# New places in PSUM for the values' sums, the gate's product and the transposes of an attention loop

## The chip, the cores and the metric

The kernel runs on 1 core of a Trainium2 chip. The metric is the device time of one execution in microseconds. Before the change it is 406.52 us, the median of 3 runs (405.61 to 407.78).

## The reference

Three layers follow each other: attention with a bias computed from positions, a mixture of experts with one expert per token, and a two-layer network with the gate h * cos(h). What matters here is the attention and the choice of the expert:

```python
scores = q @ k.T / sqrt(64) + bias                # 2 sequences, 8 heads, 576 x 576
attn = softmax(scores)                            # exp(scores - max) / (sum + 1e-9)
x = attn @ v                                      # rows of 512: 8 heads of 64
logits = x @ w_gate                               # 8 experts
gate_w = softmax(logits)[argmax]                  # one weight per row
out[i] = gate_w[i] * expert(x[i])
```

## The kernel before

**Tiling.** The attention is done in 36 steps. A step is one block of 128 query rows and one pair of heads; four steps make a block, and there are nine blocks (four of each sequence, and one in which each sequence has 64 rows). Steps are software-pipelined by hand: `step_of(n)` (line 804) issues, in this order on each engine, work of several steps. Per step n:

- `emit_exp(n, 1)` (L402, ScalarE): the exponential of the second head's scores;
- `emit_qk(n + 1, 0)` and `emit_qk(n + 1, 1)` (L385, TensorE): the next step's scores for the first and the second head, then `emit_sum` (L393, VectorE), which adds the bias and takes the minimum;
- `emit_tr(n, 0..2)` (L416, TensorE): nine 128x128 blocks of the exponentials are transposed in three groups of three, and `emit_tev(n, 0..2)` (L423, ScalarE) copies each group to SBUF; between the second and the third group stands `emit_nat(n - 2)` (L460), one more transpose, which `emit_nrm(n - 2)` (L467, VectorE) reads;
- `run_late`: pieces of the routing of a finished block (see below); `go_on` ends what they began;
- `bias_half(g, 0)` (L341 TensorE, L342 ScalarE): half of a group of rows of the bias for a later block, in steps 0 to 25; the passes L317 of VectorE (L315 of ScalarE in the first steps) prepare it;
- `emit_exp(n + 1, 0)` (L402), then in steps 27 to 31 a conversion of weights (L705, ScalarE);
- `emit_pv(n - 1)` (L434, TensorE): the values' sums, and `emit_xs(n - 1)` (L444, ScalarE), the copy of them to SBUF;
- `bias_half(g, 1)`.

**The eight PSUM banks** of the loop. Line 217 allocates `xb`, `bb`, `t0`, `t1`, one bank each, and line 220 the two score tiles `sa` and `sb`, two banks each (one for each half of 288 score columns; columns 288 to 511 of each bank are unused). `next_s` hands `sb` to the first head and `sa` to the second. `next_t` hands `t0` and `t1` in turn to the groups of transposes, so with three groups per step the third takes the bank of the first. The fourth quarter of such a bank takes the transpose of `emit_nat`, and the small products of the routing (`late_ps`). `xb` holds the values' sums, in two slots that alternate by step, and the gate's product of `f1` beside them (columns 256 to 383). `bb` holds the bias halves, and after the last of them, from step 25 on, the products of the routing (`own`).

**The routing of a block** (`finish_block`, line 494): `f1` multiplies by the gate's weights (L503 TensorE, L505 ScalarE), `f2` transposes the result and finds the best expert (L509, L512 to L522), `f3` takes the exponential (L536, ScalarE), and `f4` computes the gate's weight (L542, L543, VectorE) and multiplies the 512 columns of the rows with it (L549, VectorE). They wait in the list `late`; `run_late` (line 663) takes one piece a step before `emit_tev(n, 2)`, and `f3` and `f4` ahead of the next piece. For the first eight blocks this falls inside the loop (`f4` in steps 7, 11, 15, 20, 24, 27, 31 and 33), for the last one behind it, where `aux[0]` has become VectorE. Then `route` sends the rows to the experts' lists (L600, GpSimd).

At the end of step 34 `part_banks` gives the four score banks to the experts' sums; in step 35 `turned` transposes the first expert's rows into them.

Of the kernel before, what the change touches and what calls it, by code (L numbers as in the profile page):

```python
# [14 lines left out]
AF = mybir.ActivationFunctionType  # L15
ALU = mybir.AluOpType
# [7 lines left out]
DM = H * D  # L24
# [78 lines left out]
def attention_moe_kernel(  # L103
    ctx: ExitStack, tc: tile.TileContext,
    qd, kd, vp, small, ttab, wg, mw1, mw2, win, wout, out, dbg=None,
):
    nc = tc.nc
    V, A, P, T, Y = nc.vector, nc.scalar, nc.gpsimd, nc.tensor, nc.sync
# [85 lines left out]
    HS = S // 2  # L194
# [22 lines left out]
    xb, bb, t0, t1 = (banks.tile([128, 512], F32, name=n) for n in ("xb", "bb", "t0", "t1"))  # L217
    sst = ExitStack()
    scores = sst.enter_context(tc.tile_pool(name="scores", bufs=1, space=PSUM))
    s_bank = [scores.tile([128, 2, 512], F32, name=n) for n in ("sa", "sb")]  # L220
    t_bank = [t.rearrange("p (a c) -> p a c", a=4) for t in (t0, t1)]
    hp_w, acc_w, hp, acc = [], [t0, t1, bb], [], []

    def part_banks():
# [4 lines left out]
        hp.extend(t[:, 0:CAP] for t in hp_w)  # L229
        acc.extend(t[:, 0:CAP] for t in acc_w)  # L230

    turn_ = {"s": 0, "t": 0}

    def next_s():
        turn_["s"] += 1
        return s_bank[turn_["s"] % 2]

    def next_t():
        turn_["t"] += 1
        return t_bank[turn_["t"] % 2]  # L240

    def consts():
        of = cut(0, 128)
# [34 lines left out]
    def v_of(b, p, a, n):  # L278
        for lo, hi, t in v_parts[b, p]:
            if lo <= a and a + n <= hi:  # L280
                return t[:, a - lo:a - lo + n]
# [83 lines left out]
    e_t, et_t, z_t, xs_t, xn_t, rz_t = {}, {}, {}, {}, {}, {}  # L365
    qk_t, mn_t, tp_t, spare = {}, {}, {}, {}
# [6 lines left out]
    def emit_qk(n, u, with_sum=True):  # L373
        b, ib, p = steps[n]
        h = 2 * p + u
        if u == 0:
            if p == 0:
                z_t[b, ib] = sm_p.tile([128, H], F32, tag="z", name="z")
            e_t[n] = e_p.tile([128, 2, S], F32, tag="e", name="e")
            mn_t[n] = sm_p.tile([128, 2], F32, tag="mn", name="mn")  # L380
        ps = next_s()
        for c, a, e in [(c, 64 * c, 64 * c + 64) for c in range(B)] if b == BOTH else [(b, 0, 128)]:
            for half in range(2):
                rows_ = slice(64 * half, 64 * half + 64)
                T.matmul(out=ps[a:e, half, 0:HS], lhsT=qt[b, ib][rows_, h, a:e], rhs=kt[c, p][rows_, u, :], start=True, stop=True)  # L385
        ps_of[n, u] = ps
        if with_sum:
            emit_sum(n, u)
# [18 lines left out]
    def emit_tr(n, g):  # L407
        b, ib, p = steps[n]
        if g == 0:
            et_t[n] = et_p.tile([128, 9, 128], F32, tag="et", name="et")  # L410
        src = e_t[n].rearrange("p u s -> p (u s)")
        spare[g] = next_t()
        ps = spare[g]
        for j in range(3):
            blk = 3 * g + j
            T.transpose(ps[:, j, :], src[:, 128 * blk:128 * blk + 128], ident[:, :])  # L416
        tp_t[n, g] = ps
        if g == 2:
            e_t.pop(n)

    def emit_tev(n, g):
        dst, ps = et_t[n][:, 3 * g:3 * g + 3, :], tp_t.pop((n, g))
        A.activation(out=dst, in_=ps[:, 0:3, :], func=AF.Copy)  # L423

    def emit_pv(n):
        b, ib, p = steps[n]
        et = et_t[n]
        et_t.pop(n)
        for c, a, e in [(c, 64 * c, 64 * c + 64) for c in range(B)] if b == BOTH else [(b, 0, 128)]:
            xo = xb[:, 128 * (n % 2) + a:128 * (n % 2) + e]  # L430
            for j in (4, 0, 1, 2, 3):
                for i in range(4):
                    u, at_ = i // 2, 512 + 32 * i if j == 4 else 64 * (4 * (i // 2) + j) + 32 * (i % 2)
                    T.matmul(  # L434
                        out=xo[32 * i:32 * i + 32], lhsT=v_of(c, p, at_, 32),
                        rhs=et[:, 4 if j == 4 else 5 * u + j, a:e], start=(j == 4), stop=(j == 3),
                    )
        if p == 0:
            xs_t[b, ib] = xs_buf[n // NP % 2]
            xn_t[b, ib] = rows[tile_of(b, ib)]  # L440

    def emit_xs(n):
        b, ib, p = steps[n]
        A.activation(out=xs_t[b, ib][:, p, :], in_=xb[:, 128 * (n % 2):128 * (n % 2) + 128], func=AF.Copy)  # L444

    def emit_rz(n):
        b, ib, p = steps[n]
# [29 lines left out]

        return [(5 * c + t, 64 * c, 64 * c + 64) for c in range(B)] if b == BOTH else [(t, 0, 128)]

    aux = [P]  # L480
    own = []

    def late_f1():
        return own[0][:, 0:128] if own else xb[:, 256:384]

    def late_ps():
        return own[0][:, 128:256] if own else spare[0][:, 3]
# [6 lines left out]
    def finish_block(b, ib):  # L494
        t = tile_of(b, ib)
        loc = {}

        xs, row, rz = xs_t[b, ib], xn_t[b, ib], rz_t[b, ib]

        def f1():  # L500
            ps = late_f1()
            for p in range(NP):
                T.matmul(out=ps[32 * p:32 * p + 32, :], lhsT=wgs[:, p, :], rhs=xs[:, p, :], start=True, stop=True)  # L503
            yield
            A.activation(out=lt_buf[:, :], in_=ps[:, :], func=AF.Copy)  # L505

        def f2():
            ps = late_ps()
            T.transpose(ps, lt_buf[:, :], ident)  # L509
            yield  # L510
            lp = sm_p.tile([128, H, E], F32, tag="lp", bufs=1, name="lp")
            V.tensor_tensor(  # L512
                out=lp.rearrange("p (q u) e -> p q u e", u=2),
                in0=ps.rearrange("p (q z e) -> p q z e", q=NP, e=E)[:, :, 0:2],
                in1=rz.rearrange("p (q u) -> p q u", u=2)[:, :, :, None].to_broadcast([128, NP, 2, E]), op=ALU.mult,
            )
            lg = sm_p.tile([128, E], F32, tag="lg", name="lg")
            V.tensor_reduce(out=lg, in_=lp.rearrange("p h e -> p e h"), axis=AX.X, op=ALU.add)
            top = sm_p.tile([128, 8], F32, tag="top", bufs=2, name="top")
            V.max(out=top, in_=lg)  # L520
            ix = sm_p.tile([128, 8], U32, tag="ix", bufs=2, name="ix")
            V.max_index(out=ix, in_max=top, in_values=lg)  # L522
            nm = sm_p.tile([128, 1], F32, tag="nm", bufs=2, name="nm")
            aux[0].tensor_scalar(out=nm, in0=top[:, 0:1], scalar1=-1.0, scalar2=None, op0=ALU.mult)  # L524
            for t_, a, e in parts_of(b, t):
                aux[0].tensor_copy(idxf[a:e, t_:t_ + 1], ix[a:e, 0:1])
                aux[0].tensor_scalar(
                    out=oh[a:e, t_, :], in0=eio[a:e, 0:E], scalar1=idxf[a:e, t_:t_ + 1], scalar2=None, op0=ALU.is_equal,
                )
            loc.update(lg=lg, nm=nm)  # L530

        def f3():
            lg, nm = loc["lg"], loc["nm"]
            ex = sm_p.tile([128, E], F32, tag="ex", bufs=2, name="ex")
            es = sm_p.tile([128, 1], F32, tag="es", bufs=2, name="es")
            A.activation(out=ex, in_=lg, func=AF.Exp, bias=nm, scale=1.0, accum_out=es)  # L536
            loc["es"] = es

        def f4():
            es = loc["es"]  # L540
            gt = sm_p.tile([128, 1], F32, tag="gt", bufs=2, name="gt")
            V.tensor_scalar(out=gt, in0=es, scalar1=1e-9, scalar2=None, op0=ALU.add)  # L542
            V.reciprocal(out=gt, in_=gt)  # L543
            P.memset(row[:, DM:RW], 0.0)
            word = row[:, DM:DM + 1].bitcast(I32)
            P.iota(word, pattern=[[0, 1]], base=128 * ib if b == BOTH else b * S + 128 * ib, channel_multiplier=1)
            if b == BOTH:
                P.tensor_scalar(out=word[64:128], in0=word[64:128], scalar1=S - 64, scalar2=None, op0=ALU.add)
            V.tensor_scalar(out=row[:, 0:DM], in0=row[:, 0:DM], scalar1=gt[:, 0:1], scalar2=None, op0=ALU.mult)  # L549
            for t_, a, e in parts_of(b, t):  # L550
                row_t[t_] = row

        late.extend([(1, f1), (1, f2)] + [(0, f3)] + [(1, choose)] * ((b, ib) == CHOOSE) + [(0, f4)])
# [119 lines left out]
        return rest_  # L673

    def go_on(rest_):
        for g in rest_:
            next(g, None)

# [107 lines left out]
    ns = len(steps)  # L786
# [17 lines left out]
    def step_of(n):  # L804

        g, nxt = RUNS.get(n), RUNS.get(n + 1)
# [3 lines left out]
        if n > 1:  # L810
            b, ib, p = steps[n - 2]
# [8 lines left out]
        if n + 1 < ns:  # L820
            b, ib, p = steps[n + 1]
# [17 lines left out]
        emit_tr(n, 2)  # L839
        begun = run_late(LATE_B.get(n, n < LATE_FROM))  # L840
        emit_tev(n, 2)
        if nxt is not None:
            bias_h(nxt, on_act=ON_ACT if n < ACT_TO else (), quads=(0, 1))
        if n in EARLY:
# [20 lines left out]
        if n == SOONER:  # L865
            b, ib, p = steps[n - 1]
# [131 lines left out]

    for n in range(ns):
        step_of(n)  # L1000
    spare[1] = next_t()
    assert not late
    emit_nat(ns - 2)
    emit_rz(ns - 1)
# [5 lines left out]
        emit_nat(ns - 1)  # L1010
        emit_nrm(ns - 1)

    spare[1] = xb.rearrange("p (a c) -> p a c", a=4)
    b, ib, p = steps[ns - 1]
    finish_block(b, ib)
    tile_done(b, ib)
# [410 lines left out]
```

## Time and profile before

| | |
|---|---|
| median of 3 runs | 406.52 us (405.61 to 407.78) |
| profiled execution, its own time | 409.39 us |
| its span, first to last instruction | 407.3 us |
| mean granted TensorE clock | 0.985 |
| TensorE matmuls, weight loads | 375.4 us (92%), 288.3 us (71%) |
| VectorE, ScalarE, GpSimd | 293.9 us (72%), 282.3 us (69%), 48.0 us (12%) |
| attention loop, first scores of step 1 to those of step 34 | 28.04 to 198.15 us |

PE is TensorE's matmuls, PEld its weight loads, DVE VectorE, ACT ScalarE, POOL GpSimd. L416 is line 416 of the kernel before. In a timeline a row has the start and the duration in microseconds, the engine, line and operation, the tile written and those read, their shapes, the number of instructions merged, and in brackets the engine's idle time before it with what ended it. Matmuls are pipelined and their ends modelled.

### The profile page before, as it was taken

The page shows a single profiled execution, that of the slowest core. Times are in us where ns is not written, and L with a number is a line of the kernel's source. Part 1 is how long each engine was busy: PE and PEld are TensorE (multiplying, and loading weights), DVE is VectorE, ACT ScalarE, POOL GpSimd, SP SyncE. Part 2 cuts the span into 40 slices and gives each one's busy share as a digit, 9 for nine tenths or more (in the row PEclk, how much of TensorE's full clock was granted, in tenths as well). Part 3 has the DMA queues.
Part 4 walks back from the last instruction along what each step waited for, and adds up shares of the span by engine and source line. Part 5 has one row for each costly group of instructions (what it writes and reads, how often), then busy time and mean ns, then how long its engine had stood idle before and what let it go on. Part 6 is the DMA issues. An engine that isn't in the chain of part 4 may idle for free. (4 is left out here: it accounts for less than half of the span.)

```text
span 407.3 us, 10577 instructions
## 1 busy us (share of the span) xinstructions
PE 375.4 (92%) x4106; PEld 288.3 (71%) x4106; DVE 293.9 (72%) x759; ACT 282.3 (69%) x633; POOL 48.0 (12%) x122
## 2 busy tenths in 40 slices
PE   8888989999999999999978989998999999899992
PEld 5335656666666666767767879964998998789971
DVE  3856566868687967589766968974687788888670
ACT  3858978888888778899864448734766666576660
POOL 2000001010101312111580202300000000000003
PEclk9999999999999999999999989999899999999997
DMA  5679755449963555689934595992022133230003
GB/s 178 173 214 259 186 163 159 124 118 251 307 187 114 167 159 165 197 266 221 376 99 170 195 193 77 326 317 74 31 62 94 65 105 141 103 106 1 2 2 127
DMA packets 47779, 63.91 MB, mean 157 GB/s; under 512 B 6756, under 2 KB 30948, under 8 KB 47721
## 3 DMA queue, kind: packets, MB, share of 16 engines
q1 hardware_dynamic: 46553, 60.67, 51.9%
q0 software_dynamic: 1168, 2.48, 1.7%
q8 instruction: 34, 0.56, 0.6%
q14 instruction: 24, 0.20, 0.2%
HBM read 41.15 MB, written 11.54 MB: 129 GB/s over the span
## 5 line engine op out<-in xcount | busy, mean ns | idle before, releaser
L423 ACT ACTIVATE et<-t 128x384 f32<-128x384 f32 x108 | 50.3, 491 | 18.1 <-PE t L416 8.8
L416 PE MATMUL t<-ident,e 128*128 128x128 f32 x324 | 52.6, 286 | 7.6 <-ACT et L423 5.3
L317 DVE TENSOR_SCALAR h<-tt,sml 128x576 f32<-128x576 f32 x123 | 57.6, 513 | 1.0 <-PE bb L341 0.9
L416 PEld LDWEIGHTS t<-ident,e 128*128 128x128 f32 x324 | 34.1, 141 | 31.0 <-ACT et L423 15.2
L402 ACT ACTIVATE e<-e,mn 128x576 f32<-128x576 f32 x72 | 55.1, 766 | 0.0
L341 PE MATMUL bb<-h,sml 128*32 128x288 f32 x448 | 38.7, 411 | 2.6 <-ACT wo L342 2.6
L342 ACT ACTIVATE wo<-bb,sml 128x288 f32<-128x288 f32 x56 | 28.1, 501 | 11.2 <-PE bb L341 9.7
L1182 PE MATMUL t<-yh,s1h 128*128 128x384 f32 (+1 forms) x88 | 27.8, 316 | 2.2 <-DVE tn L1281 1.8
L434 PEld LDWEIGHTS xb<-et,wi 128*32 128x32 f32 x1000 | 25.0, 110 | 6.3 <-ACT wo L505 2.7
L434 PE MATMUL xb<-et,wi 128*32 128x128 f32 (+1 forms) x1000 | 29.3, 263 | 0.0
L1182 PE MATMUL t<-yl,s1h 128*128 128x384 f32 (+1 forms) x88 | 27.6, 313 | 0.1
L1182 PE MATMUL t<-yh,s1l 128*128 128x384 f32 (+1 forms) x88 | 27.5, 312 | 0.0
L385 PE MATMUL sb<-k,q 64*128 64x288 f32 (+1 forms) x160 | 27.1, 449 | 0.1
L1274 DVE TENSOR_TENSOR tn<-tn,kn 128x640 f32<-128x640 f32 (+2 forms) x18 | 13.5, 752 | 18.4 <-ACT kn L1271 18.4
L393 DVE CUSTOM_DVE_ANT_0 e<-sb,keep 128x576 f32<-128x576 f32 x16 | 12.1, 756 | 20.4 <-PE sb L385 17.4
L385 PE MATMUL sa<-k,q 64*128 64x288 f32 (+1 forms) x160 | 23.7, 405 | 0.5 <-DVE bias L359 0.5
L1284 ACT ACTIVATE gh<-tn 128x640 fp32r<-128x640 f32 (+2 forms) x18 | 12.0, 679 | 15.4 <-DVE tn L1281 15.2
L524 POOL TENSOR_SCALAR nm<-top 128x1 f32<-128x1 f32 x8 | 1.9, 234 | 161.7 <-DVE top L520 151.7
L385 PEld LDWEIGHTS sb<-k,q 64*128 64x128 f32 (+1 forms) x160 | 10.5, 174 | 14.6 <-issue 6.9
L1247 POOL DMA_INDIRECT out_dram<-o,id x5 | 4.9, 976 | 132.5 <-ACT o L1246 131.3
L951 PE MATMUL hp<-xh,s1h 128*128 128x288 f32 x64 | 19.5, 305 | 0.0
L1182 PEld LDWEIGHTS t<-yh,s1h 128*128 128x128 f32 x88 | 16.8, 191 | 3.4 <-DVE tn L1281 2.4
(274 smaller groups left out, 1004.1 us busy)
## 6 DMA issues: line engine op xcount, KB each, us to landing
keep<-win SPq DMA_DIRECT2D x16, 512.0 KB, 4.4
keep<-wout SPq DMA_DIRECT2D x16, 512.0 KB, 3.5
w1r<-mw SPq DMA_DIRECT2D x12, 512.0 KB
w2r<-mw SPq DMA_DIRECT2D x12, 512.0 KB, 8.3
disp<-wo SPq DMA_DIRECT2D x10, 516.0 KB, 5.4
bias<-wo SPq DMA_DIRECT2D x16, 288.0 KB, 4.1
q<-qd SPq DMA_DIRECT2D x8, 512.0 KB, 4.9
k<-kd SPq DMA_DIRECT2D x8, 288.0 KB, 5.9
```

The costliest lines, as they stand in the source:

```text
L317: V.tensor_scalar(out=h, in0=win_, scalar1=col, scalar2=0.0, op0=ALU.add, op1=ALU.max)
L341: T.matmul(out=ps[32 * j:32 * j + 32, :], lhsT=w2s, rhs=h_t[g, j][:, c0:c0 + 288], start=True, stop=True)
L342: A.activation(out=ev_t[g][:, c0:c0 + 288], in_=ps, func=AF.Copy, scale=rst[:, g:g + 1])
L385: T.matmul(out=ps[a:e, half, 0:HS], lhsT=qt[b, ib][rows_, h, a:e], rhs=kt[c, p][rows_, u, :], start=True, stop=True)
L393: V.tensor_tensor_reduce(out=e_t[n][:, u].rearrange("p (a c) -> p a c", a=2), in0=ps[:, :, 0:288], in1=bias_of(ib, h).rearrange("p (a c) - ...
L402: A.activation(out=e_t[n][:, u], in_=e_t[n][:, u], func=AF.Exp, scale=-1.0, bias=mn_t[n][:, u:u + 1], accum_out=z_t[b, ib][:, h:h + 1],)
L416: T.transpose(ps[:, j, :], src[:, 128 * blk:128 * blk + 128], ident[:, :])
L423: A.activation(out=dst, in_=ps[:, 0:3, :], func=AF.Copy)
L434: T.matmul(out=xo[32 * i:32 * i + 32], lhsT=v_of(c, p, at_, 32), rhs=et[:, 4 if j == 4 else 5 * u + j, a:e], start=(j == 4), stop=(j == 3),)
L951: T.matmul(out=ps, lhsT=a[g % 3][:, k], rhs=x[:, k], start=(k == 0 and i == 0), stop=(k == 3 and i == 2))
L1182: T.matmul(out=sums(f, i), lhsT=w[f % 3][:, k], rhs=ya[k][x][:, o0 + a:o0 + e], start=(k == 0 and n == 0), stop=(k == 3 and n == 2),)
L1274: V.tensor_tensor(out=tn, in0=tn, in1=kn, op=ALU.subtract)
```

## The change

The third group of transposes gets a bank of its own, `xb` (in the last step the groups use `t0`, `t1`, `t0` as before). The sums of the values leave `xb` for columns 288 to 415 of the first bank of `sa`, one slot for all steps but the last two, which stay in `xb`. The gate's product moves to the same columns of the first bank of `sb`, up to the time at which the routing uses `bb`. The multiply L549 is taken off VectorE for the blocks in the loop and put on ScalarE, where it is issued after `emit_tev(n, 2)`, or at the next `go_on`.

```diff
-    t_bank = [t.rearrange("p (a c) -> p a c", a=4) for t in (t0, t1)]
+    t_bank = [t.rearrange("p (a c) -> p a c", a=4) for t in (t0, t1, xb)]
...
-    turn_ = {"s": 0, "t": 0}
+    turn_, s_of = {"s": 0}, {}
...
-        ps = next_s()
+        ps = s_of[u] = next_s()
...
-        spare[g] = next_t()
+        spare[g] = t_bank[g if n < ns - 1 else g % 2]
...
+    def sum_of(n):
+        return s_of[1][:, 0, HS:HS + 128] if n < ns - 2 else xb[:, 128 * (n % 2):128 * (n % 2) + 128]
...
-            xo = xb[:, 128 * (n % 2) + a:128 * (n % 2) + e]
+            xo = sum_of(n)[:, a:e]
...
-        A.activation(out=xs_t[b, ib][:, p, :], in_=xb[:, 128 * (n % 2):128 * (n % 2) + 128], func=AF.Copy)
+        A.activation(out=xs_t[b, ib][:, p, :], in_=sum_of(n), func=AF.Copy)
...
-        return own[0][:, 0:128] if own else xb[:, 256:384]
+        return own[0][:, 0:128] if own else s_of[0][:, 0, HS:HS + 128]
...
-            V.tensor_scalar(out=row[:, 0:DM], in0=row[:, 0:DM], scalar1=gt[:, 0:1], scalar2=None, op0=ALU.mult)
+            if aux[0] is V:
+                V.tensor_scalar(out=row[:, 0:DM], in0=row[:, 0:DM], scalar1=gt[:, 0:1], scalar2=None, op0=ALU.mult)
+            else:
+                put_off.append(lambda: A.activation(out=row[:, 0:DM], in_=row[:, 0:DM], func=AF.Copy, scale=gt[:, 0:1]))
...
     def go_on(rest_):
+        while put_off:
+            put_off.pop(0)()
...
         emit_tev(n, 2)
+        while put_off:
+            put_off.pop(0)()
...
-    spare[1] = next_t()
+    spare[1] = t_bank[1]
...
-    spare[1] = xb.rearrange("p (a c) -> p a c", a=4)
+    spare[1] = t_bank[2]
```

## Rows read from the trace of the kernel before

**Rows 1.** Stretches: length, busy us (instructions) of PE, PEld, DVE, ACT, POOL, granted clock, DMA share, GB/s

```profile
28.04:56.61 28.57, 25.52 (x344) 15.06 (x345) 18.56 (x51) 25.23 (x59) 0.00 (x0) 1.00 0.80 214
56.61:164.39 107.78, 104.17 (x1814) 69.58 (x1810) 81.76 (x263) 87.94 (x226) 12.59 (x38) 1.00 0.61 174
164.39:198.15 33.76, 32.13 (x495) 23.35 (x491) 27.77 (x95) 30.02 (x80) 4.97 (x20) 1.00 0.93 256
```

**Rows 2.** Timeline of a step without routing work, 73.2 to 78.3 us

```profile
73.65 0.75 DVE L393 CUSTOM_DVE_ANT_0 e<-sa,bias 128x576 f32<-128x576 f32 x1
73.83 0.88 ACT L423 ACTIVATE et<-t 128x384 f32<-128x384 f32 x2 [0.41 <-ACT e L402]
73.91 0.27 PE L460 MATMUL t<-ident,wo 128*128 128x128 f32 x1
74.38 0.55 PE L416 MATMUL t<-ident,e 128*128 128x128 f32 x3 [0.19 <-ACT et L423]
74.96 0.49 ACT L423 ACTIVATE et<-t 128x384 f32<-128x384 f32 x1 [0.25 <-PE t L416]
75.36 1.27 PE L434 MATMUL xb<-et,wo 128*32 128x128 f32 x40
75.67 0.51 ACT L342 ACTIVATE wo<-bb,sml 128x288 f32<-128x288 f32 x1 [0.21 <-PE bb L341]
76.07 0.77 ACT L402 ACTIVATE e<-e,mn 128x576 f32<-128x576 f32 x1
76.82 0.27 ACT L444 ACTIVATE wo<-xb 128x128 f32<-128x128 f32 x1
77.05 0.76 PE L385 MATMUL sb<-k,q 64*128 64x288 f32 x4
78.22 0.87 PE L416 MATMUL t<-ident,e 128*128 128x128 f32 x6
```

**Rows 3.** Groups by line: busy us, mean ns, then idle before and its releasers

```profile
L416 PEld LDWEIGHTS t<-ident,e 128*128 128x128 f32 x324 | 34.1, 141 | 31.0 <-ACT et L423 15.2 <-issue 7.5 <-ACT wo L342 3.3
...
L434 PEld LDWEIGHTS xb<-et,wi 128*32 128x32 f32 x1000 | 25.0, 110 | 6.3 <-ACT wo L505 2.7 <-issue 0.7
...
L705 ACT ACTIVATE wi<-keep 128x512 f32<-128x512 f32 x16 | 10.6, 664 | 0.0
...
L549 DVE TENSOR_SCALAR wo<-wo,gt 128x512 f32<-128x512 f32 x9 | 4.4, 487 | 0.3
```

**Rows 4.** Timeline of step 33: a third group of transposes that does not wait

```profile
195.57 0.49 PE L416 MATMUL t<-ident,e 128*128 128x128 f32 x3
```

**Rows 5.** Timeline of step 0: second scores that wait, and the transposes behind them

```profile
28.71 0.30 PEld L385 LDWEIGHTS sa<-k,q 64*128 64x128 f32 x4 [0.38 <-DVE mn L393]
...
29.40 1.07 PE L416 MATMUL t<-ident,e 128*128 128x128 f32 x6
```

**Rows 6.** Timeline of step 7, in which a block's rows are multiplied

```profile
70.19 0.16 DVE L543 RECIPROCAL gt<-gt 128x1 f32<-128x1 f32 x1
...
70.64 0.50 ACT L342 ACTIVATE wo<-bb,sml 128x288 f32<-128x288 f32 x1 [0.21 <-PE bb L341]
...
71.43 0.67 PE L341 MATMUL bb<-h,sml 128*32 128x288 f32 x8
```

**Rows 7.** Timeline of step 31, with a multiply and a conversion, and no bias work

```profile
188.12 0.16 DVE L543 RECIPROCAL gt<-gt 128x1 f32<-128x1 f32 x1
188.21 0.77 ACT L402 ACTIVATE e<-e,mn 128x576 f32<-128x576 f32 x1
...
188.94 0.76 PE L385 MATMUL sb<-k,q 64*128 64x288 f32 x4
...
189.53 0.26 ACT L444 ACTIVATE wo<-xb 128x128 f32<-128x128 f32 x1
```

**Rows 8.** Stretches of the experts' stage around a fall of the clock, columns as above

```profile
238.00:240.00 2.00, 0.77 (x6) 0.53 (x5) 0.84 (x2) 0.47 (x1) 0.00 (x0) 1.00 0.99 245
...
242.00:244.00 2.00, 2.00 (x10) 2.00 (x9) 2.00 (x6) 2.00 (x6) 0.00 (x0) 0.50 0.74 62
```

More of the change, by code (lines that the diff above doesn't have):

```diff
@@ L236, in next_s @@
         return s_bank[turn_["s"] % 2]
-    def next_t():
-        turn_["t"] += 1
-        return t_bank[turn_["t"] % 2]
     def consts():
@@ L478, in parts_of @@
         return [(5 * c + t, 64 * c, 64 * c + 64) for c in range(B)] if b == BOTH else [(t, 0, 128)]
-    aux = [P]
+    aux, put_off = [P], []
     own = []
     def late_f1():
-        return own[0][:, 0:128] if own else xb[:, 256:384]
+        return own[0][:, 0:128] if own else s_of[0][:, 0, HS:HS + 128]
     def late_ps():
```

## The prediction

> **What bounds the kernel now.** I read the table of stretches first, for what each engine does between the first score matmul and the end of the attention loop. In steps 5 to 25 (107.78 us, 21 steps, 5.13 us each) TensorE is busy 104.17 us and ScalarE 87.94; in steps 26 to 33 (33.76 us, 8 steps, 4.22 each) 32.13 and 30.02, all at a granted clock of 1.00 [rows 1]. TensorE carries the loop, with ScalarE close behind. The reader is to see that what a wait of TensorE costs is worth having back, but that ScalarE has only about 0.9 us a step to spare.
>
> Then the timeline of one step without extra work, from 73.2 to 78.2 us [rows 2]. The third group of transposes starts at 74.38 although TensorE had issued the block before it at 73.91. It waits for the first eviction, which starts at 73.83 and takes 0.49 like the one at 74.96: 74.32, and a hop of 0.06. Three transposes that do not wait take 0.49 in all, and each of them 0.27, so they are 0.11 apart [rows 2, 4]; three that wait take 0.55. Without the wait the group runs from 74.02 to 74.51 and not to 74.93: 0.42 us of TensorE. The groups by line say that this is the rule: the loads of the transposes sat idle 31.0 us, 15.2 of them for the eviction [rows 3].
>
> Last I looked for what is held per bank and not per column. The values' sums wait 2.7 us in all for the copy of the gate's product, which reads other columns of the same bank [rows 3]. So two users of one bank take turns, and the new places have to be costed by bank.
>
> **The change part by part.** The profiled execution took 409.39 us, 2.87 above the median of the three runs (406.52); the sum is made on 409.39 and its difference taken off the median.
>
> *Three banks for the transposes.* Group 2 goes to a bank whose last reader was the third eviction a whole step earlier, so its wait goes. I read the gap in each of the 21 steps 5 to 25: 0.29 to 0.35 us beyond the free spacing (0.36 in the step shown), to which the faster group adds 0.06. Five of these steps are also those of the multiply, counted below; the other 16 give 0.38 on average, 6.1 us. What is late next? ScalarE's third eviction (74.96) could follow its second at once, some 0.35 earlier; the bias eviction (75.67), the exponential (76.07) and the copy of the sums (76.82) wait for TensorE or follow in order, so all move by the same amount and the step closes 0.38 shorter. ScalarE needs about 4.1 us of the 4.7 that stay. Steps 0 to 4 have ScalarE busy 25.23 of 28.57 us [rows 1]: there it is the limit, 0.67 us of idle a step. I take 0.8 for all five, between 0 and 5 × 0.42 = 2.1.
>
> *The sums move from two alternating slots of one bank to a single slot in the second score tile's first bank.* Two waits are new. The sums of step n-1 must wait until VectorE has read the second score tile: that read ends at 73.65 + 0.75 = 74.40, the sums start at 75.36 [rows 2], about 74.95 after the change. Covered by 0.5 us; if VectorE falls behind by more, that is a price on TensorE one for one. And the second head's score matmul must wait until the copy of the sums (76.82 + 0.27 = 77.09, with a hop 77.15) has left that bank. A score matmul that waits at its own start has the next transposes 0.69 us behind it [rows 5], while now the transposes follow the first head's scores by 78.22 - 77.05 = 1.17. So the copy is in time up to 77.05 + 0.48 = 77.53, a slack of 0.38, and both sides move together: nothing lost in a plain step. Queued behind that wait on TensorE are the transposes, and behind them ScalarE's evictions. The bounds are 0 and the 0.42 that the step gains.
>
> *The gate's product* goes to the first score tile. The sums no longer wait for its copy: 6 steps, 2.7 us of idle weight loads, of which only what the matmuls did not cover counts, an estimate of 0.07 each, 0.4 us; between 0 and 2.7. The first head's next scores come a full step later, so no wait takes its place.
>
> *The multiply by the gate weight moves from VectorE to ScalarE, after the third eviction,* in 8 of 9 blocks. VectorE loses 8 × 0.487 [rows 3]; it idles for scores in most steps, so I count nothing for that. ScalarE has no such row; the nearest is a 128x512 pass from SBUF to SBUF at 664 ns, of which some 0.57 are taken from the next instruction (they overlap by about 0.1). In the step of 70 us the reciprocal ends at 70.35, the multiply runs from 70.40 to 70.97, and the bias eviction, which now starts at 70.64, starts then; it is over at 71.47, and the second bias half, which now starts at 71.43 and would have started near 71.0, waits until 71.5 [rows 6]. So these five steps gain nothing and lose 0.09: +0.45. Below: the multiply disappears in idle time, and each gains its 0.38. Above: the reciprocal comes 0.4 later, and each loses 0.5.
>
> The Trainium skill (ScalarE: Activation LUTs, Rules for kernel authors) says to give multiplications to VectorE rather than ScalarE, and budgets about 0.3 us plus 0.83 ns per element for an ACTIVATE. By it the multiply is an estimated 0.72 us, and the eight would cost 1.2 us more than in my sum. The row of 664 ns and the 487 of VectorE point the same way with a smaller difference.
>
> *Steps without bias work, 26 to 33.* There the cover between sums and second scores is gone: only the first head's scores lie between. In the five from 27 to 31 ScalarE also does a 0.66 us conversion between exponential and copy [rows 3]. In the step that leads to 188.94 the copy starts at 189.53, so it ends, with a hop, at 189.86, against a limit of 188.94 + 0.48 = 189.42 [rows 7]: 0.44 too late. That eats the 0.35 to 0.42 of the transposes: zero in steps 28 to 30. In steps 27 and 31 the multiply comes on top: the reciprocal there ends at 188.28, so the exponential moves from 188.21 to 188.90, and everything behind it by 0.69: 0.44 + 0.69 = 1.1 us lost in each, 2.2. Steps 26 and 32 have no conversion before the copy: -0.8 together. Step 33 has the eighth multiply ahead of an exponential that the second group of transposes needs: an estimate of +0.4. In step 35 the score banks are handed to the experts, and the first transposes of the dispatched rows wait for the last copy out of the bank: +0.3, between 0 and 0.8.
>
> Sum: -0.8 - 6.1 - 0.4 + 0.45 - 0.8 + 2.2 + 0.7 = -4.75 us, 404.6 for the profiled execution and **401.8** for the median. What comes after the loop starts earlier by that; it is not touched.
>
> **The rivals.**
> *The multiply is hidden.* Then the five steps gain 5 × 0.38 instead of losing 0.45 (2.35 more), steps 27 and 31 lose nothing, nor does step 33: 2.35 + 2.2 + 0.4 = 4.95 more, 396.8. For it: ScalarE idles twice in a plain step (0.41 and 0.21) [rows 2]. Against it: none of that idle time lies between the multiply and the copy of the sums.
> *The change does not do what it says:* the transposes stream, but half of what they gain is taken by the next wait of the same step, the exponential or VectorE's passes. The 6.5 of transposes and gate's product become 3.2: 405.1. For it: the early steps, where ScalarE is the limit. Against it: the plain step's idle rows.
> *Slower, by the copy of the sums.* Place: the second head's score matmul. If the copy comes later by d than I read, each late step (9 of them) pays d, and each plain one pays what exceeds 0.38. At d = 0.45 the gain is gone (9 × 0.45 = 4.0, 16 × 0.07 = 1.1); at 0.6 the late steps cost 5.4 and the plain ones 3.5: +4.2, 410.7. For it: the copy stands last but two in ScalarE's order, behind the exponential, and two engines then take turns on one chain. Against it: 0.38 of slack in the row.
> *The clock.* At 242 to 244 us the granted clock was 0.50, the 1.2 GHz level, and 10 matmuls ran in 2.00 us; shortly before, at 238 to 240, TensorE was busy for 0.77 of 2.00 us at the full 2.4 GHz [rows 8]. Where such stretches fall is not the change's doing; one more or less is an estimated 1.5 us either way, and goes into the range.
>
> **How the numbers follow.** Forecast 0.52, the multiply hidden 0.14, half the gain 0.20, slower 0.14. A measurement of this kernel can tell about 0.5%, 2.0 us, from no change. So faster 0.66, same 0.20, slower 0.14. The range leaves out the slower case and the far end of the hidden multiply: 397.8 to 405.9, the forecast with its bounds (0.8 at the hand-over, 5 × 0.4 at the multiply, 1.3 in the early steps, 1.5 of clock) inside it.
>
> **What would show it.** In the changed kernel's trace the third group of transposes follows the block before it by 0.11 us in steps 5 to 25, and the 15.2 us of idle loads for the evictions are nearly gone. Plain steps take 4.6 to 4.7 us, those with the multiply still 5.1. The weight loads of the second score tile show a new wait for the copy of the sums, from step 27 on and hardly before; 27 and 31 take 5.1. I am wrong if that wait stands in every step, if the sums wait for VectorE's score reads, or if the plain steps stay at 5.0 with another wait in the place of the old one.

## The result and the profile after

The changed kernel takes **401.39 us** (median of 4 runs, 400.66 to 401.89); the kernel before took 406.06 beside it. The ratio is 0.988, with a 95% interval of 0.984 to 0.992. The forecast was 401.8, with a range of 397.8 to 405.9. Run again beside more runs of the kernel before, the changed kernel came to 0.990 (0.986 to 0.994).

The profiled execution took 400.66 us. First the table of stretches of the kernel after, cut like [rows 1] (steps 0 to 4, 5 to 25, 26 to 33; a step is cut here at the first head's scores that it issues, which are those that the next step works on); the columns are length, busy us (instructions) of PE, PEld, DVE, ACT and POOL, granted clock, DMA share, GB/s:

```profile
27.07:54.75 27.68, 25.54 (x344) 15.09 (x344) 18.75 (x51) 24.63 (x59) 0.00 (x0) 1.00 0.80 221
54.75:156.75 102.00, 100.52 (x1813) 70.35 (x1809) 79.30 (x258) 87.95 (x231) 12.69 (x38) 1.00 0.65 183
156.75:192.53 35.78, 32.17 (x496) 23.11 (x492) 26.99 (x93) 30.30 (x81) 5.06 (x20) 1.00 0.92 256
```

Against [rows 1] the first stretch is 0.89 us shorter, the second 5.78 shorter, and the third 2.02 *longer*: 4.65 in all, and the medians differ by 4.67. So the loop won in its first 26 steps and gave a part back in the last eight. That the two differences agree so closely is in part luck: step 34, which these stretches leave out, gives back another 1.2 us (shown below), and the profiled executions differ by 8.73 us. Of the 4.08 us that are not in the three stretches, 0.97 lie ahead of the loop, where a second execution of the kernel after shows none of it (28.12 against 28.04 us at the start); the rest lies mostly behind it (see the last section).

Where it was won: the same step as in [rows 2], a step without routing work, in the timeline of the kernel after.

```profile
71.06 0.75 DVE L389 CUSTOM_DVE_ANT_0 e<-sa,bias 128x576 f32<-128x576 f32 x1
71.39 0.87 ACT L419 ACTIVATE et<-t 128x384 f32<-128x384 f32 x2 [0.42 <-PE t L412]
71.46 0.27 PE L459 MATMUL t<-ident,wo 128*128 128x128 f32 x1
71.56 0.49 PE L412 MATMUL xb<-ident,e 128*128 128x128 f32 x3
72.15 0.49 ACT L419 ACTIVATE et<-xb 128x384 f32<-128x384 f32 x1
72.50 1.28 PE L433 MATMUL sa<-et,wo 128*32 128x128 f32 x40
72.80 0.50 ACT L338 ACTIVATE wo<-bb,sml 128x288 f32<-128x288 f32 x1 [0.15 <-PE bb L337]
73.96 0.26 ACT L443 ACTIVATE wo<-sa 128x128 f32<-128x128 f32 x1
74.19 0.76 PE L381 MATMUL sb<-k,q 64*128 64x288 f32 x4
```

The third group starts 0.10 us behind the block before it (71.56 against 71.46; 0.47 in [rows 2]) and takes 0.49. VectorE's read of the second score tile ends at 71.81, and the sums follow at 72.50: no wait there. The copy of the sums ends at 74.22, before the second head's scores want the tile. The step takes 4.62 us and took 5.02.

Where it was given back: the multiplication in step 7, then the one at the end of step 27 and what follows it in step 28, then the eighth one, in step 34. Timeline of the kernel after:

```profile
67.79 0.73 ACT L551 ACTIVATE wo<-wo,gt 128x512 f32<-128x512 f32 x1
68.42 0.48 ACT L338 ACTIVATE wo<-bb,sml 128x288 f32<-128x288 f32 x1
68.95 0.69 PE L337 MATMUL bb<-h,sml 128*32 128x288 f32 x8 [0.35 <-ACT wo L338]
...
163.89 0.72 ACT L551 ACTIVATE wo<-wo,gt 128x512 f32<-128x512 f32 x1
164.18 0.76 PE L381 MATMUL sb<-k,q 64*128 64x288 f32 x4
164.52 0.76 ACT L398 ACTIVATE e<-e,mn 128x576 f32<-128x576 f32 x1
165.28 0.65 ACT L709 ACTIVATE wi<-keep 128x512 f32<-128x512 f32 x1
165.83 0.25 ACT L443 ACTIVATE wo<-sa 128x128 f32<-128x128 f32 x1
166.14 0.76 PE L381 MATMUL sa<-k,q 64*128 64x288 f32 x4 [1.20 <-ACT wo L443]
...
192.86 0.72 ACT L551 ACTIVATE wo<-wo,gt 128x512 f32<-128x512 f32 x1 [0.42 <-DVE gt L542]
...
194.91 0.44 PE L412 MATMUL t<-ident,e 128*128 128x128 f32 x2 [0.55 <-ACT e L398]
...
197.93 0.71 PE L935 MATMUL hp<-ident,xg 96*128 96x96 f32 x6 [0.40 <-ACT wo L443]
```

In step 7 the bias eviction comes 0.63 us later than it could, and TensorE waits for it. In step 28 multiplication, exponential and conversion stand in one row on ScalarE, the copy of the sums is fourth, and TensorE stands still until it is done. In step 34 the multiplication stands ahead of the exponential that the second group of transposes needs, and the expert's first transposes (L935), which go into the score banks, wait for the copy of the sums. The groups by line say how often the second scores wait (busy us, mean ns, idle before and its releasers); PEld waits for that copy 10 times: 1.66 us in step 28, 0.65, 0.60 and 0.54 in steps 29 to 31, 1.71 in step 32, and five times 0.15 to 0.40 elsewhere:

```profile
L412 PEld LDWEIGHTS t<-ident,e 128*128 128x128 f32 x219 | 23.2, 141 | 16.1 <-issue 13.1 <-ACT e L398 1.3 <-ACT et L419 0.7
...
L381 PEld LDWEIGHTS sa<-k,q 64*128 64x128 f32 (+1 forms) x160 | 12.6, 175 | 10.6 <-ACT wo L443 6.7 <-DVE bias L355 0.9 <-DVE mn L389 0.4
...
L551 ACT ACTIVATE wo<-wo,gt 128x512 f32<-128x512 f32 x8 | 5.8, 724 | 0.9 <-DVE gt L542 0.7
```

The 15.2 us of idle loads for the evictions in [rows 3] are now 0.7.

### The profile page after: what moved, and what is told of

Read it like the earlier page. It is cut to its first block, busy times and chain, and to the rows that moved or that the text cites. A ratio compares the mean times of both kernels' runs of the same rounds, so it can differ in the third digit from the quotient of the medians.

```text
span 398.9 us, 10628 instructions
## 1 busy us (share of the span) xinstructions
PE 367.1 (92%) x4106; PEld 284.5 (71%) x4106; DVE 290.3 (73%) x751; ACT 282.3 (71%) x641; POOL 47.9 (12%) x122
## 5 line engine op out<-in xcount | busy, mean ns | idle before, releaser
L337 PE MATMUL bb<-h,sml 128*32 128x288 f32 x448 | 39.6, 412 | 4.1 <-ACT wo L338 4.0
L419 ACT ACTIVATE et<-t 128x384 f32<-128x384 f32 x73 | 32.7, 490 | 14.2 <-PE t L412 13.0
L412 PEld LDWEIGHTS t<-ident,e 128*128 128x128 f32 x219 | 23.2, 141 | 16.1 <-issue 13.1
L412 PE MATMUL t<-ident,e 128*128 128x128 f32 x219 | 33.0, 283 | 1.2 <-ACT e L398 0.6
L433 PE MATMUL sa<-et,wi 128*32 128x128 f32 (+1 forms) x1000 | 29.4, 262 | 0.2 <-issue 0.2
L433 PEld LDWEIGHTS sa<-et,wi 128*32 128x32 f32 x1000 | 25.6, 110 | 5.6 <-DVE mn L389 0.8
L381 PE MATMUL sa<-k,q 64*128 64x288 f32 (+1 forms) x160 | 24.5, 415 | 3.3 <-ACT wo L443 2.7
L381 PEld LDWEIGHTS sa<-k,q 64*128 64x128 f32 (+1 forms) x160 | 12.6, 175 | 10.6 <-ACT wo L443 6.7
```

The source lines that it names most:

```text
L337: T.matmul(out=ps[32 * j:32 * j + 32, :], lhsT=w2s, rhs=h_t[g, j][:, c0:c0 + 288], start=True, stop=True)
L433: T.matmul(out=xo[32 * i:32 * i + 32], lhsT=v_of(c, p, at_, 32), rhs=et[:, 4 if j == 4 else 5 * u + j, a:e], start=(j == 4), stop=(j == 3),)
```

## The experiments

Each experiment ran in five rounds beside the kernel before. The table has the length of two stretches of the loop in each profiled execution (from the starts of the first head's scores, like [rows 1]; 107.78 and 33.76 before, all at a granted clock of 1.00) and the ratio to the kernel before with its interval. Two executions of the kernel after agree in these stretches within 0.05 us, so they tell single waits apart; the ratios don't tell differences under about 0.7%. What a step before 34 shifts into step 34 is not in these stretches.

| kernel | steps 5 to 25 | steps 26 to 33 | ratio |
|---|---|---|---|
| after | 102.00 | 35.78 | 0.988 (0.984 to 0.992) |
| after, again | 101.99 | 35.83 | 0.990 (0.986 to 0.994) |
| after, two transposes banks | 107.83 | 37.03 | 1.014 (1.009 to 1.020) |
| after, two banks, product on VectorE | 107.06 | 35.73 | 1.005 (1.001 to 1.009) |
| before, product on ScalarE | 108.57 | 34.51 | 1.011 (1.005 to 1.016) |
| after, product on VectorE | 99.76 | 34.37 | 0.987 (0.981 to 0.993) |
| after, product later on ScalarE | 100.81 | 34.75 | 0.990 (0.984 to 0.996) |
| after, conversion later | 101.99 | 32.90 | 0.986 (0.982 to 0.990) |
| after, late sums with the routing in the bias bank | 102.00 | 36.67 | 0.997 (0.994 to 1.001) |
| after, late sums alone in the bias bank | 102.02 | 34.37 | 0.989 (0.985 to 0.993) |
| product on VectorE + conversion later | 99.76 | 32.89 | 0.975 (0.971 to 0.979) |
| product on VectorE + late sums alone | 99.77 | 33.31 | 0.980 (0.975 to 0.985) |
| all three | 99.77 | 33.51 | 0.977 (0.972 to 0.982) |

The expectations are in us against 401.4 for the kernel after; the kernel before took 406.6, 410.0, 407.5 and 407.4 us in the four sets, which ran on three chips, so the totals are compared as ratios.

("Product" here is the multiplication of a block's rows by the gate's weight.)

**What wins: two banks again.** The kernel after, with the groups taking `t0` and `t1` in turn as before; the sums and the gate's product stay in the score banks.

```diff
-    t_bank = [t.rearrange("p (a c) -> p a c", a=4) for t in (t0, t1, xb)]
+    t_bank = [t.rearrange("p (a c) -> p a c", a=4) for t in (t0, t1)]
...
-        spare[g] = t_bank[g if n < ns - 1 else g % 2]
+        spare[g] = next_t()
```

> The kernel after, with the transposes' groups again in two banks taken in turn; the sums stay in the second head's score bank, the gate's product in the first head's. Theory: the third group waits again for the copy of the first, 0.4 us in each of some 33 steps, so the gain is gone and the waits for the copy of the sums stay: 406 to 411, by plain steps of about 5.0 us. Rival (what gains is that the sums and the gate's product left their bank, the third transposes bank being hidden by other work): stays at 401 to 402.5, plain steps at 4.6 to 4.7.

The same with the multiplication on VectorE, which leaves only the move of sums and gate's product:

> The kernel with the transposes' groups in two banks and the sums and the gate's product in the score banks, and the multiplication by the gate back on VectorE: what is left is the move of the sums and of the product alone, against the kernel before. Theory (the move alone gains 0.1 us in six steps and loses in the late ones, where the second head's scores wait for the copy of the sums): plain steps 5.02-5.03 us as before, steps 7, 11, 15 and 24 at 5.03 instead of 5.16, steps 26 to 33 at 35 to 36.5 us against 33.8 before: 1 to 2.5 us slower than before, 1.002 to 1.008. Rival (the late loss with two banks is the multiplication's on ScalarE, not the sums'): steps 26 to 33 at 34 us or less, 0.997 to 1.001.

And the kernel before with only the multiplication on ScalarE:

> The kernel before, with one edit: a block's values are multiplied by the gate on ScalarE, behind the third group's copy. Theory: dearer by about 0.1 us in five steps and by 0.5 to 1.2 us in steps 27 and 31 and 33: 407 to 409. Rival (VectorE's relief gains): below 406, down to 403.

Stretches of these three, in this order, columns as above:

```profile
55.78:163.61 107.83, 104.23 (x1813) 69.99 (x1809) 80.00 (x258) 90.01 (x231) 12.79 (x38) 1.00 0.62 174
163.61:200.64 37.03, 33.41 (x495) 22.84 (x491) 27.24 (x93) 31.21 (x81) 5.04 (x20) 1.00 0.90 260
```

```profile
55.66:162.72 107.06, 103.43 (x1813) 70.18 (x1809) 81.72 (x263) 87.76 (x226) 12.58 (x38) 1.00 0.62 175
162.72:198.45 35.73, 33.49 (x496) 22.84 (x492) 28.07 (x95) 29.85 (x80) 4.97 (x20) 1.00 0.94 260
```

```profile
55.54:164.11 108.57, 104.95 (x1813) 69.39 (x1809) 80.02 (x258) 90.30 (x231) 12.84 (x38) 1.00 0.61 172
164.11:198.62 34.51, 32.19 (x496) 23.34 (x492) 26.88 (x93) 31.10 (x81) 5.07 (x20) 1.00 0.95 257
```

Without the third bank the whole kernel is slower than before. Plain steps are back at 5.02 to 5.03 us, and the loads of the transposes wait for the evictions again, 13.9 us in 34 waits. So the third bank is the gain; the move is what it takes, and the multiplication on ScalarE only costs. The rival that the move itself gains falls, but for 0.72 us; so does the one that relieving VectorE gains. Read as differences, in steps 5 to 25 the move of sums and gate's product is worth 107.06 - 107.78 = -0.72, which is 0.12 in each of the six steps with a gate's product; the multiplication +0.77 or +0.79; in steps 26 to 33 the move costs 35.73 - 33.76 = **+1.97** and the multiplication +1.30 on top, where alone it costs 34.51 - 33.76 = +0.75.

**What gives back in the steps to 25: the multiplication.** Back on VectorE in the kernel after:

```diff
-            if aux[0] is V:
-                V.tensor_scalar(out=row[:, 0:DM], in0=row[:, 0:DM], scalar1=gt[:, 0:1], scalar2=None, op0=ALU.mult)
-            else:
-                put_off.append(lambda: A.activation(out=row[:, 0:DM], in_=row[:, 0:DM], func=AF.Copy, scale=gt[:, 0:1]))
+            V.tensor_scalar(out=row[:, 0:DM], in0=row[:, 0:DM], scalar1=gt[:, 0:1], scalar2=None, op0=ALU.mult)
```

> The kernel after, with the multiplication of a block's values by the gate back on VectorE. Theory (the third bank brings the gain, ScalarE's multiplications give part of it back): steps 7, 11, 15, 20 and 24 shrink from 5.11-5.17 us to about 5.03 or less, and steps 28 and 32 lose part of their 5.12 and 5.67 us; total 0.6 + 0.7 to 1.5 us off 401.4, so about 399.7 (398.8 to 400.4). Rival (the relief of VectorE, 0.5 us per multiplication, is itself a gain): slower than 401.4, by up to 8 x 0.5 = 4 us, so 402 to 405.

```profile
54.76:154.52 99.76, 99.61 (x1813) 70.35 (x1809) 81.07 (x263) 85.10 (x226) 12.75 (x38) 1.00 0.67 188
154.52:188.89 34.37, 31.96 (x496) 22.96 (x492) 27.88 (x95) 28.93 (x80) 4.97 (x20) 1.00 0.95 265
```

TensorE is now busy 99.61 of 99.76 us; the 0.15 that are left are a wait in step 10, in which a transpose of the routing waits for an eviction. Steps 7, 11, 15 and 24 fall by 0.55 or 0.56 each (5.16 to 4.61 in step 7) and step 20 by 0.28; step 10 takes 0.28 back. Without and with the third bank, both with the multiplication on VectorE (107.06 against 99.76), that bank is worth 7.30 us in the 21 steps, 0.35 a step. The total moved less than the loop: 3.6 us shorter to step 34, and a ratio that can't be told from that of the kernel after. Where that went is in the last section, and not settled.

On ScalarE, but behind the copy of the sums:

```diff
         emit_tev(n, 2)
-        while put_off:
-            put_off.pop(0)()
...
             emit_xs(n - 1)
+        while put_off:
+            put_off.pop(0)()
```

> The kernel after, with the multiplication by the gate issued on ScalarE behind the copy of the sums instead of behind the third group's copy (a block's tokens are sent on behind it in any case). Theory (what a multiplication costs in a plain step is the bias eviction and the exponential queued behind it on ScalarE, as the bias matmuls wait for the eviction): steps 7, 11, 15 and 24 fall from 5.13-5.17 to 4.6-4.85 us, 1 to 2 us off the start of step 26, nothing won or lost behind it beyond 1 us; 0.982 to 0.986 of the kernel before. Rival (ScalarE's total work in the step, 0.6 us more wherever it stands): the five steps stay at 5.1 us, 0.988.

Step 7 is at 4.61, but step 8 now takes 4.86 instead of 4.61: the multiplication delays the next exponential, and four of the five cost 0.24 to 0.29 us where they cost 0.55. Half of it was its place, half is ScalarE's time. In steps 20 and 27 and for the eighth block this edit moves nothing, because the block's rows are sent on before the copy and the multiplication has to stand ahead of that; step 28 keeps its 5.12 us, and step 32 falls to 4.63 us. The ratio shows nothing of the 2.2 us.

**What gives back from step 26 on.** Two theories: the second head's scores wait for the copy of the sums, whose bank they share; or ScalarE is full in these steps, whatever the order. First the conversion's first instruction goes behind the second head's exponential:

```diff
         if n > 0:
             emit_exp(n, 1)
+        if n in EARLY:
+            early_ops.pop(0)()
...
-        if n + 1 in EARLY:
-            early_ops.pop(0)()
```

> The kernel after, with the first instruction of a weight piece's conversion (0.65 us on ScalarE, in steps 27 to 31) issued behind the next step's second-head exponential instead of between the first-head exponential and the copy of the sums. Theory (the second head's scores wait for the copy of the sums, which stands in ScalarE's queue behind the conversion): the waits of 0.54 to 0.65 us vanish, those of 1.66 and 1.71 us fall to about 1.0; 0.3 us off each of three steps and 0.6 us off two, 1 to 2 us in all: 399.4 to 400.4. Rival (ScalarE as a whole is the bound of the late steps, whatever the order): no change, 401 to 402.

The late steps take 32.90 us instead of 35.78, with the same work on every engine: the order was the cost. In steps 29 to 31 the wait for the copy falls to the 0.17 that the loads also show in step 27; in steps 28 and 32, where the multiplication still stands ahead of the copy, TensorE waits 0.65 and 0.40 us for it:

```profile
165.03 0.76 PE L381 MATMUL sa<-k,q 64*128 64x288 f32 x4 [0.65 <-ACT wo L443]
```

Then the sums of the late steps in the bias bank, which the bias no longer uses:

```diff
-        return s_of[1][:, 0, HS:HS + 128] if n < ns - 2 else xb[:, 128 * (n % 2):128 * (n % 2) + 128]
+        return s_of[1][:, 0, HS:HS + 128] if not own else bb[:, 256 + 128 * (n % 2):384 + 128 * (n % 2)] if n < ns - 2 else xb[:, 128 * (n % 2):128 * (n % 2) + 128]
```

> The kernel after, with the sums of steps 26 on in two slots of the bias bank, which the bias has left by then (columns 256 to 511; the gate's product and its turning have columns 0 to 255 there as before). Theory (the second head's scores wait for the copy of the sums, 1.66 and 1.71 us in steps 27 and 31, 0.54 to 0.65 in others, and that is what the late steps lose): the waits go, and 1 to 2.5 us with them: 399 to 400.4. Rival (ScalarE's queue itself holds the late steps, the waiting scores are only its shadow): no change, 401 to 402.

That was a miss, 0.9 us *more*. The timeline of this kernel shows why: the bias bank also holds the small products of the routing, and the sums now wait until VectorE or ScalarE has read those (L656 and L504), though they are other columns.

```profile
168.51 0.16 DVE L656 CUSTOM_DVE_ANT_0 cnt<-bb,gone 128x8 f32<-128x8 f32 x1
168.74 1.30 PE L433 MATMUL bb<-et,wo 128*32 128x128 f32 x40 [0.94 <-DVE some L656]
...
172.91 0.29 ACT L504 ACTIVATE wo<-bb 128x128 f32<-128x128 f32 x1
173.26 0.43 PE L433 MATMUL bb<-et,wi 128*32 128x128 f32 x8 [0.46 <-ACT wo L504]
```

So the same with the routing's products left where they are in the earlier steps, and `own` filled only at the end of step 33 (the sums go to `bb` from n = 25 on):

> The kernel after, with the sums of steps 25 to 33 in columns 256 to 511 of the bias bank, which then holds nothing else until step 33: the gate's product stays in the first head's score bank and the small late results stay in the first transposes bank. Theory (the sums were held up in the kernel with everything in the bias bank by VectorE's late reads of that bank, and without them the move takes away the second head's wait for the copy of the sums): steps 26 to 32 at 3.7 to 4.3 us, 1 to 2.5 us off the whole: 399 to 400.4. Rival (the busy ScalarE holds the late steps in any case, or VectorE's late reads now hold up the first transposes bank): 401 to 405.

Steps 26 to 32 take 28.56 us against 30.71 after; step 33 rises from 5.07 to 5.81, since the gate's product now stands in the first score tile there and TensorE waits 0.67 us for VectorE's read. No second score waits for a copy any more, and steps 29 to 31 are down by 0.32 to 0.36 us each. But steps 28 and 32 still take 4.78 and 4.80 us. There the second group of transposes now waits for the second head's exponential, which stands behind the same multiplication and conversion; from step 28:

```profile
166.62 0.44 PE L412 MATMUL t<-ident,e 128*128 128x128 f32 x2 [0.84 <-ACT e L398]
```

So the wait for the copy is the cause in the steps with a conversion alone, where each cure takes it away by itself. In the two that also follow a multiplication, ScalarE's queue is late for both of its readers, and the copy is only the first to show it; how much order and load each have there is not taken apart. In the totals neither shows beyond its interval (0.986 and 0.989).

**Together.** With the multiplication on VectorE: the conversion later, the late sums alone, or all three.

> The kernel after, with the conversion's first instruction behind the second-head exponential and the multiplication by the gate on VectorE. Theory: 2.2 us less to the start of step 26 as without the move of the conversion, and all late waits for the copy of the sums gone, steps 26 to 33 at 33 us or less (34.4 with the multiplication alone moved, 35.8 after): 2.2 + 2.8 us off, 396 to 398. Rival (ScalarE's queue as a whole): as with the multiplication alone, 399.5 to 400.5.

> As the kernel with the late sums alone in the bias bank, and with the multiplication by the gate on VectorE. Theory: 2.2 us less to the start of step 26, late steps at 33 us in all against 35.8: 396 to 398.5. Rival (late reads hold up the first transposes bank): steps 26 to 33 over 34.4, 400 or more.

> The kernel after with all three edits: multiplication on VectorE, the conversion's first instruction behind the second-head exponential, the sums of steps 25 to 33 alone in the bias bank. Theory (each of the three takes away its own wait of the late steps): steps 26 to 33 at 32 us or less, below the 32.9 of the first two edits and the 33.3 of the first and third; 0.97 to 0.975 of the kernel before. Rival (with the conversion moved, the copy of the sums is never late, so the bank no longer matters): 32.9 us or more, 0.975 to 0.98.

> The kernel after, unchanged, on the chip on which the next two run. Both theories: 0.988 of the kernel before, as in its first comparison (0.984 to 0.992); its late steps 26 to 33 at 35.8 us again.

The conversion's move needs no new bank, and with the multiplication on VectorE it has the shortest loop: 0.975 of the kernel before, with an interval that lies below that of the kernel after, though not apart from those of the other two. Its late steps come to the same with the multiplication on either engine (32.90 and 32.89), but by two differences that cancel. Step 28 takes 4.57 us with it on ScalarE and 3.81 on VectorE; step 32 takes 4.32 and 5.04. On VectorE the multiplication and the conversion's passes delay that engine's read of the second score tile, and the values' sums, which share its bank, wait for it. Step 32 of the kernel with the product on VectorE and the conversion later:

```profile
179.52 0.75 DVE L389 CUSTOM_DVE_ANT_0 e<-sa,bias 128x576 f32<-128x576 f32 x1
...
180.33 1.63 PE L433 MATMUL sa<-et,wi 128*32 128x128 f32 x40 [0.99 <-DVE mn L389]
```

All three together are not better than two (33.51 late, against an expected 32 or less), as the rival had it: the two cures remove the same wait, and the bank's costs step 33 (5.79 us for 5.07). On the chip of the repeat, all three took 397.74 us where the kernel after took 403.62.

## Why the prediction was right, and where not

**The third bank: right.** Forecast -0.8 for steps 0 to 4; measured -0.89. Forecast 16 steps × 0.38 = 6.1 and 0.4 for the gate's product; the 16 steps fell by 6.38 together. The two banks show that all of it but 0.72 is the bank, so 5.66 for 6.1. No other wait took its place, as the reading of [rows 2] had it.

**The gate's product: twice too small.** Forecast 0.4 for six steps, measured 0.72, all of it in those steps (5.31 to 5.19). The wait in [rows 3] was on the path for 0.12 each, not 0.07.

**The five multiplications: right.** Forecast +0.45, measured +0.59 (5.16 for 5.02 in step 7). The nearest row gave 0.57 us until the next instruction; L551 starts its successor 0.63 later and takes 0.72. That last is the figure that the Trainium skill (ScalarE: Activation LUTs, Rules for kernel authors) gives by its budget, and its rule to leave multiplications to VectorE is borne out by 2.24 us of the loop to step 26 (102.00 against 99.76). The prediction's 1.2 us for the eight by that budget set the whole 0.72 against the 0.57 until the next instruction; by the 0.63 it is 0.5.

**The late steps: the wait right, its cost too small by 0.6.** The forecast for steps 26 to 32 is -0.8 + 2.2 = +1.4; steps 26 to 33 measured +2.02, and step 33 has no part in it (-0.01). The steps are cut at the first head's scores, so a copy that is late in step 27 shows in step 28: the text's "27 and 31 take 5.1" are 28 (5.12 us) and 32 (5.67), and its two steps without a wait are 26 and 27. These gave -0.73 for a forecast -0.8; the three with a conversion alone +0.11, +0.05 and -0.01 for a forecast zero. The two with multiplication and conversion gave +1.06 and +1.54 for 1.1 each. The second head's scores start 1.96 and 2.01 us behind the first head's there, where the kernel before has 0.59 (188.94 and 189.53). Against the prediction's limit of 0.48 they are 1.48 and 1.53 too late, for a forecast 0.44 + 0.69 = 1.13; in the three others 0.36 to 0.47, for 0.44. The forecast also forgot to set the bank's gain of about 0.4 in the same step against the 1.13; the two errors cancel in step 28. In step 32 the values' sums take 1.79 us (185.73 to 187.52) and not 1.30; the records name no engine for that gap, which is most of the 0.6.

**The eighth multiplication: right in kind, too small.** Forecast +0.4, by an exponential that the second group of transposes needs. The prediction put it in step 33; the multiplication runs at 192.86, 0.33 us into step 34, and that wait is there (0.55 us at 194.91). From the first scores of step 34 to the values' sums it is 2.99 us before, 2.99 with the product on VectorE, and 3.70 after: +0.71.

**The hand-over: right in kind.** Forecast +0.3, by a wait of the first transposes of the dispatched rows for the last copy. From the first scores of step 34 to these transposes it is 4.22 us before, 4.68 with the product on VectorE, and 5.40 after. Less the 0.71 or so of the multiplication that is +0.46. Where the stop of the last section falls on this copy it costs more: 7.33 us in the second execution of the kernel after. To the first expert's matmul the times (8.44 before, 8.18 and 11.34 after) don't tell, since they differ more between two executions of one kernel than between the kernels.

**The sum.** From the first scores of the loop to the first transposes of the dispatched rows the profiled kernel after is 3.47 us shorter (174.33 and 170.86 us), where the forecast for these places is 4.75. The late steps were undersized by 0.6, the eighth multiplication by 0.3, the hand-over and the five multiplications by about 0.15 each. The medians moved by 4.67. So the steps of the prediction are borne out, but that the total came within 0.4 us of it is luck in part: by these two profiles 1.2 us of the 4.67 did not come from the places that it speaks of.

**The rivals.** The multiplication is not hidden; VectorE's version beats it by 2.2 us in the loop to step 26. Half the gain taken by the next wait: no, 6.4 of 6.5. Slower by the copy of the sums: the mechanism is real, but it decides only where the bias work no longer lies between sums and scores; in the plain steps the slack read in [rows 2] held. The prediction's other sign of being wrong, sums that wait for VectorE's read of the scores, hardly shows in the kernel after; it does where the multiplication is back on VectorE, in step 32 (0.54 us, and 0.99 with the conversion later).

## What to carry to other kernels

A tile's bank is shared by whoever uses its free columns: before putting something there, list who reads the other columns, when, and how late each of them can be. Here the same free columns cost nothing in 21 steps and 2 us in eight, because in the eight the reader of the bank stood behind an exponential, a conversion and twice a multiplication in its engine's queue. Moving one 0.65 us instruction behind another then gave back more than a further bank did. A sum that stays the same when work moves from one engine to another can be two differences that cancel: compare step by step. And a bank that frees the busiest engine of a wait is worth the wait times the steps, if what lies next has slack.

## What else the runs showed

**A 2.4 us stop of ScalarE that no engine explains.** The copy of the sums in step 34, in the two profiled executions of the same kernel after (timeline; the first row is the first execution):

```profile
197.60 0.28 ACT L443 ACTIVATE wo<-sa 128x128 f32<-128x128 f32 x1 [0.48 <-PE sa L433]
```

```profile
200.62 0.28 ACT L443 ACTIVATE wo<-sa 128x128 f32<-128x128 f32 x1 [2.41 <-remote]
```

In the second, the matmuls of the sums that it copies had ended at 198.62, 2.0 us earlier. A wait of 1.99 to 2.44 us with this mark stands before the copy in step 34, or before the last copy behind the loop, in six of the fourteen profiles: those of the kernel before, of after (second time), of both kernels with two banks, of the later conversion and of the later product. In after (first time), product on VectorE, and product on VectorE with the later conversion no copy there waits over 0.6 us. In before with the product on ScalarE and in both kernels with late sums in the bias bank the copy in step 34 is as late (2.27 to 2.36 us idle), with an expert's transposes named, whose result it does not read. So it stands there in seven of the eight profiles with the product on ScalarE; in the six with it on VectorE that copy waits 0.5 to 1.7 us. With one profile each, and one kernel that shows both, that may be chance. What ScalarE waits for is open: no run here tests it.

**The clock behind the loop.** After a stretch in which TensorE was busy for 1.67 of 4 us, the second execution of the kernel after has stretches of lower clock (columns as above; PE is the first busy column):

```profile
198.00:202.00 4.00, 1.67 (x31) 1.40 (x24) 0.00 (x0) 1.45 (x6) 3.20 (x10) 0.84 0.40 133
202.00:206.00 4.00, 3.80 (x26) 3.56 (x25) 2.08 (x5) 2.96 (x8) 3.56 (x12) 0.73 0.00 0
238.00:242.00 4.00, 4.00 (x25) 4.00 (x24) 3.21 (x7) 3.44 (x9) 0.00 (x0) 0.57 1.22 78
282.00:286.00 4.00, 3.84 (x16) 3.64 (x17) 1.68 (x3) 2.20 (x7) 0.00 (x0) 0.58 0.25 87
```

The first execution has none before its last matmuls, and took 400.66 us against 406.20, with the same loop to 0.05 us. Of the difference 1.05 us lie ahead of the loop, 3.16 between the first scores of step 34 and the first expert's matmul (the stop, and a stretch of lower clock behind it), and 1.4 behind that. In the kernel before there were two, near 242 and near 286 us. So one profile's total against another's is no measure of a change here: the stretches of the loop are, and the medians. Of what the runs with shorter loops lost behind it, stop, clock and, with the product on ScalarE, the 0.71 us of the eighth multiplication are the visible part; their totals follow the loop within 3 us, and how much of that is chance the runs do not settle.
